# Two chained MLPs after a long convolution: the first MLP 20 tiles ahead of the second, weight decoding and GpSimd sums moved to other steps

## The chip, the cores and the metric

The kernel runs on one core of one Trainium2 chip. The metric is device time in microseconds (us): 2869.82 us, the median of three runs (2868.83 to 2870.09).

## The reference, cut to what matters

```
u = x * v;  h_filt = (relu(pos_emb @ w1) @ w2) * window
y = irfft(rfft(u, 2S) * rfft(h_filt, 2S))[:S];  a = x * y        # long convolution, S = 12480, 2 batches
g = h * clip(h + 3, 0, 6) / 6,   h = a @ w_in1;   b = g @ w_out1   # MLP 1, 24960 tokens, 128 -> 2048 -> 128
out = relu(b @ w_in2)**2 @ w_out2                                 # MLP 2, same sizes
```

All inputs are float32. The kernel is handed the four MLP weights as 64-bit words and makes float32 pairs of them on the chip ("decoding").

## The kernel before, in words

The first 497 us hold the filter MLP and the convolution, built as matrix products of a two-level Fourier transform. Their last level (`s4`, lines 451 to 464) is done tile by tile in the MLP part, which is the rest of the kernel and the part that is changed.

The 24960 tokens are 64 tiles of 390 tokens. Both MLPs go through all tiles; a tile of one MLP takes eight steps (q = 0 to 7), each with 256 of the 2048 hidden units. A list fixes the order of the steps (lines 478 to 486): MLP 1 (l = 0) starts AHEAD = 10 tiles early, then tiles of MLP 1 and MLP 2 (l = 1) alternate, and the last tiles are of MLP 2 alone. One loop (lines 612 to 639) issues each step's work to all engines; every engine runs its own instructions in the order in which they were issued.

One step is:
- `l1` (line 504): six matmuls, 128x128 weights by 390 tokens, into a PSUM tile `ph`. All operands are split in a high and a low part, so each product is three matmuls.
- `relu` (ScalarE, `r`) and `act` (VectorE, `g`, lines 531 and 534).
- `split`, one step later: ScalarE copies the high part `gh` (line 541), and VectorE or GpSimd subtracts for the low part `gl` (line 544). In the first 8*AHEAD steps VectorE takes this at q = 0, 3, 6 and GpSimd at the other five; after that VectorE has 0, 2, 4, 6.
- `l2`, three steps later (LAG): six matmuls into `acc`, the last two with `gl`.

`g` and `r` have two buffers each: the activation of step n can't write `g` before the split of step n-2 has read it. `acc` and the convolution's `py` share two PSUM buffers.

Around these: `finish` (line 568) takes a tile's result out of `acc`. For MLP 1 it makes the high part `xh` on ScalarE and the low part `xl` on VectorE (line 574), which wait in AHEAD + 1 buffers until MLP 2 comes to that tile. `combine` (line 433) makes the sums and differences for the convolution's last level: four GpSimd instructions, issued together at q = 5 of an MLP 1 tile while MLP 1 is alone, and at q = 2 of an MLP 2 tile later. `loads` issues the four DMAs of a later tile on SyncE's queue. `gate` and `gate_split` multiply by x and make `oh`, `ol` (line 475).

`late` (line 598) is a generator that decodes the weights still missing: 3 items are left of one part of the first output weights, 10 of another, and then for each weight of MLP 2 a DMA and 12 items of waiting, and four parts of 10 items: 117 items. Of a part's ten items eight are VectorE instructions on 512 columns (lines 100 to 119) and two are ScalarE's alone. The loop takes items ahead of `relu` and `act`: two a step up to n = 13, then five in four steps. They must be done when MLP 2 starts, at n = 88.

Of the kernel before, what the change touches and what calls it, by code (L numbers as in the profile page):

```python
# [7 lines left out]
F32 = mybir.dt.float32  # L8
F32R = mybir.dt.float32r
U32 = mybir.dt.uint32  # L10
AF = mybir.ActivationFunctionType
ALU = mybir.AluOpType
# [15 lines left out]
NT = 64  # L28
TOK = 390
# [10 lines left out]
def tile_hyena_moe(ctx: ExitStack, tc, xg, vg, xT, pos, w1d, w2d, win, fmat, twc,  # L40
                   tws, dcs, inv, vtab, w_in1, w_out1, w_in2, w_out2, out):
    nc = tc.nc
# [85 lines left out]
    def decode_split(w, part):  # L128
        for _ in parts.pop((w, part)):
            pass  # L130


    def tile_loads(j, za, zb, v, x):
        nc.sync.dma_start(v, vtab[j])
        nc.sync.dma_start(x, xT[j])
        nb = NBLK - (j == 0)
        for h, t in enumerate((za, zb)):
            zr = zds[0][h, j] if j < ZA else zds[1][h, j - ZA]
            nc.sync.dma_start(t.rearrange("k d r b c -> k d (r b c)")[:, :nb],
                              zr[:nb].rearrange("d k c -> k d c"))  # L140
# [215 lines left out]
    with tc.tile_pool(name="cv_ps", bufs=4, space=PSUM) as vps:  # L356
# [17 lines left out]
        for i in range(NI + 2):  # L374
# [26 lines left out]
            if i == NI - 1:  # L401
# [12 lines left out]
                za, zb = (room0[:K1, k].rearrange("k (d r b c) -> k d r b c", d=NBLK, r=2, b=2) for k in (0, 1))  # L414
# [8 lines left out]
    zt, pm, xin = {0: (za, zb)}, {}, {}  # L423

    def loads(j):
        za = mo.tile([K1, NBLK, 2, 2, 16], F32, name=f"za{j}", tag="za")
        zb = mo.tile([K1, NBLK, 2, 2, 16], F32, name=f"zb{j}", tag="zb")
        vt[j] = mo.tile([K1, 2, 2, N1], F32, name=f"vt{j}", tag="vt")
        xt[j] = mo.tile([128, TOK], F32, name=f"xt{j}", tag="xt")
        tile_loads(j, za, zb, vt[j], xt[j])  # L430
        zt[j] = (za, zb)

    def combine(j):
        za, zb = zt.pop(j)
        pp = mo.tile([K1, 2, 2, D], F32, name=f"pp{j}", tag="pp")
        pn = mo.tile([K1, 2, 2, D], F32, name=f"pn{j}", tag="pn")
        pm[j] = (pp, pn)

        p, n = (t.rearrange("k r b (d c) -> k d r b c", d=NBLK) for t in (pp, pn))
        if j == 0:  # L440
            for t, z in ((p, za), (n, zb)):
                for r in range(2):
                    nc.scalar.activation(t[:, :, r], z[:, :, r], AF.Copy)
            return
        for t, op in ((p, ALU.add), (n, ALU.subtract)):
            for r in range(2):
                nc.gpsimd.tensor_tensor(t[:, :, r], za[:, :, r], zb[:, :, 1 - r], op)  # L447

    py, ob = {}, {}

    def s4(j):

        ps = mps.tile([128, 512], F32, name=f"py{j}", tag="acc", bufs=2)
        v = vt.pop(j)
        for u in range(4):
            q, b = divmod(u, 2)
            o, n = UOFF[u]
            for r in range(2):
                nc.tensor.matmul(ps[:, o:o + n], pm[j][q][:, r, b, :],  # L459
                                 v[:, q, r, :n], start=(r == 0), stop=(r == 1))  # L460
                if u == 3 and r == 1:
                    pm.pop(j)
                    py[j] = ps
                yield

    def gate(j):
        ob[j] = mo.tile([128, TOK], F32, name=f"o{j}", tag="o")
        nc.vector.tensor_tensor(ob[j], py.pop(j)[:, :TOK], xt.pop(j), ALU.mult)

    def gate_split(j):  # L470
        o = ob.pop(j)
        h = mo.tile([128, TOK], F32R, name=f"oh{j}", tag="oh")
        l = mo.tile([128, TOK], F32R, name=f"ol{j}", tag="ol")
        nc.scalar.activation(h, o, AF.Copy)
        nc.vector.tensor_tensor(l, o, h.bitcast(F32), ALU.subtract)  # L475
        xin[(0, j)] = (h, l)

    AHEAD = 10
    order = []
    for j in range(NT + AHEAD):  # L480
        if j < NT:
            order.append((0, j))
        if j >= AHEAD:
            order.append((1, j - AHEAD))
    NP = NFC // 2
    steps = [(l, j, q) for l, j in order for q in range(NP)]
    LAG = 3
    QS = 4
    filling = {}

    def between(n, place):
# [6 lines left out]

        for _ in range(2 if j < AHEAD else place % 2):
            if "s4" in filling and next(filling["s4"], True):  # L500
# [3 lines left out]
    def l1(n):  # L504
        l, j, q = steps[n]
        xh, xl = xin[(l, j)]
        ps = mps.tile([128, 2, 512], F32, name=f"ph{n}", tag="ph", bufs=3)
        assert (2 * l, q // 2) in ready
        w = wh[2 * l]
        for c in range(2):  # L510
            f = 2 * q + c
            sl = slice(128 * f, 128 * f + 128)
            for m, (wt, x) in enumerate(((w[:, 1, sl], xh), (w[:, 0, sl], xl),
                                         (w[:, 0, sl], xh))):
                nc.tensor.matmul(ps[:, c, :TOK], wt, x, start=(m == 0), stop=(m == 2))  # L515
            between(n, c)
        ph[n] = ps
# [19 lines left out]
    def split(n):  # L537
# [3 lines left out]
        nc.scalar.activation(h, g, AF.Copy)  # L541
        on_vector = (0, 3, 6) if n < 8 * AHEAD else (0, 2, 4, 6)
        eng = nc.vector if steps[n][2] in on_vector else nc.gpsimd
# [3 lines left out]
    def l2(n):  # L547
        l, j, q = steps[n]
        if q == 0:
            acc[(l, j)] = mps.tile([128, 512], F32, name=f"acc{l}_{j}", tag="acc", bufs=2)  # L550
        ps = acc[(l, j)][:, :TOK]
        w = wh[2 * l + 1]
        h, lo = gh.pop(n)
        assert (2 * l + 1, q // 2) in ready
        ops = []
        for part, x in ((1, h), (0, h), (0, lo)):
            for c in range(2):
                f = 128 * (2 * q + c)
                ops.append((w[:, part, f:f + 128], x[:, c]))
        for m, (wt, x) in enumerate(ops):  # L560
            nc.tensor.matmul(ps, wt, x, start=(q == 0 and m == 0),  # L561
                             stop=(q == NP - 1 and m == len(ops) - 1))
            if m % 3 == 2:
                between(n + LAG, 2 + m // 3)
        if q == NP - 1:
            xin.pop((l, j))

    def finish(l, j):
        ps = acc.pop((l, j))[:, :TOK]
        if l == 0:  # L570
            h = mr.tile([128, TOK], F32R, name=f"xh{j}", tag="xh", bufs=AHEAD + 1)
            lt = mr.tile([128, TOK], F32R, name=f"xl{j}", tag="xl", bufs=AHEAD + 1)
            nc.scalar.activation(h, ps, AF.Copy, scale=1.0 / 6.0)
            nc.vector.scalar_tensor_tensor(lt, ps, 1.0 / 6.0, h.bitcast(F32),
                                           ALU.mult, ALU.subtract)
            xin[(1, j)] = (h, lt)
        else:
            ot = mr.tile([128, TOK], F32, name=f"ot{j}", tag="ot")
            nc.scalar.activation(ot, ps, AF.Copy)
            nc.scalar.dma_start(out[j], ot)  # L580

    loads(1)
    write(NBLK - 1, 1, tail.pop(), nc.sync)
    loads(2)
    staged.close()
    mr = ctx.enter_context(tc.tile_pool(name="moe2", bufs=2, side="right"))
    combine(0)
    for _ in s4(0):
        pass
    gate(0)  # L590
    gate_split(0)
    combine(1)
    decode_split(1, 0)
    for _ in range(2):
        next(parts[(1, 1)])
# [2 lines left out]
    def late():  # L598
        yield from parts.pop((1, 1))
        yield  # L600
        yield from decoding(None, 1, 2)
        yield
        for w in (2, 3):
            raw_weight(w)
            for _ in range(12):
                yield
            for part in range(4):
                yield from decoding(mr, w, part)
                yield

    rest = late()
    for n in range(len(steps) + LAG + 1):
        if n < len(steps):
            l, j, q = steps[n]
            l1(n)
        m = n - LAG
        if 0 <= m < len(steps):
            l2(m)
        if 0 <= m - 1 < len(steps) and steps[m - 1][2] == NP - 1:
            finish(*steps[m - 1][:2])  # L620
        if n < len(steps):
            if l == 0 and j < AHEAD and QS < q < QS + 3:
                (gate if q == QS + 1 else gate_split)(j + 1)
            if l == 1 and j + AHEAD + 1 < NT and q < 2:
                (gate_split if q else gate)(j + AHEAD + 1)
            for _ in range(2 if n < 14 or n % 4 == 0 else 1):
                next(rest, None)
            relu(n)
            act(n)
        if 0 <= n - 1 < len(steps):  # L630
            split(n - 1)
        if n < len(steps):

            t, at = (j, QS + 1) if l == 0 else (j + AHEAD, 2)
            if t < AHEAD or l == 1:
                if q == at and t + 2 < NT:
                    combine(t + 2)
                if q == at + 1 and t + 3 < NT:
                    loads(t + 3)


def _tables():
# [88 lines left out]
```

## Time and profile before

| | |
|---|---|
| median of three runs | 2869.82 us |
| the profiled execution | 2869.38 us, span 2867.6 us |
| TensorE busy with matmuls | 2779.6 us (97%), 15712 matmuls |
| VectorE / ScalarE / GpSimd busy | 2122.8 / 2006.1 / 1570.8 us |
| mean granted clock of TensorE | 0.991 |

Busy time is the time in which an engine has an instruction in work; a matmul's end is modelled. In the views, PE is TensorE (PEld its weight loads), DVE is VectorE, ACT is ScalarE, POOL is GpSimd and SP is SyncE; a trailing q is the engine's queue. L544 is line 544 of the kernel before. Windows are in us from the start of the span. An idle time is put down to what ended it, so "PEld acc <- POOL gl" is TensorE's time of waiting for GpSimd's `gl`.

### The profile page before, as it was taken

To read this page: it belongs to the slowest core of one execution; us is meant where nothing else is said; L and a number is where in the kernel's file an instruction comes from. 1 tells how busy PE (TensorE), PEld (TensorE's weight loads), DVE (VectorE), ACT (ScalarE), POOL (GpSimd) and SP (SyncE) were. 2 spreads that over 40 slices of the span, in tenths; PEclk is the share of its full clock that TensorE was granted. 3 is DMA by queue.
4 is the path that set the end of the run, shared out by engine and by line. 5 is a ranking of instruction groups with operands and counts; after the bars stand their busy time and mean duration, and the time that the engine had idled before them with its cause. 6 is when DMAs were issued, how large, how long until landed. Compare 5 with 4: busy or idle time off the path is not lost.

```text
span 2867.6 us, 42099 instructions
## 1 busy us (share of the span) xinstructions
PE 2779.6 (97%) x15712; PEld 2711.9 (95%) x15712; DVE 2122.8 (74%) x2280; ACT 2006.1 (70%) x2630; POOL 1570.8 (55%) x1020
## 2 busy tenths in 40 slices
PE   7999998888999999999999999999999999999999
PEld 5888887778999999999999999999999999999999
DVE  6888888899877777777777777777777777777666
ACT  6445445666777777777777777777777777777776
POOL 4888885655455555555555555555555555554444
PEclk9999999999999999999999999999999999999999
DMA  4343433321011111111110111111111111110000
GB/s 158 103 137 106 140 108 88 101 60 30 24 27 26 26 26 27 26 26 26 26 27 24 26 26 27 26 26 26 26 26 26 26 26 27 26 26 6 10 12 15
DMA packets 139419, 125.77 MB, mean 44 GB/s; under 512 B 99692, under 2 KB 122702, under 8 KB 137806
## 3 DMA queue, kind: packets, MB, share of 16 engines
q1 hardware_dynamic: 128322, 89.23, 11.4%
q10 hardware_dynamic: 10892, 33.86, 4.0%
q8 instruction: 123, 2.02, 0.3%
q14 instruction: 82, 0.67, 0.1%
HBM read 86.64 MB, written 36.37 MB: 43 GB/s over the span
## 4 chain that ended last, share of the span: by engine, by line
PE 83%; DVE 7%; issue 5%; ACT 2%; POOL 2%; DMA 0%; POOLq 0%; ACTq 0%; DVEq 0%
PE acc L561 36%; PE ph L515 36%; PE p L217 4%; PE py L459 3%; PE p L178 2%; PE p L248 1%; DVE g L531 1%; ACT h L331 1%; DVE a L194 1%; POOL l L203 1%; DVE b L188 1%; DVE p L192 1%; DVE wa L106 1%; DVE wa L104 0%; DVE gl L544 0%
## 5 line engine op out<-in xcount | busy, mean ns | idle before, releaser
L544 POOL TENSOR_TENSOR gl<-g,gh 128x780 fp32r<-128x780 f32 x522 | 984.2, 1885 | 1156.1 <-ACT gh L541 1151.5
L541 ACT ACTIVATE gh<-g 128x780 fp32r<-128x780 f32 x1024 | 869.1, 849 | 111.7 <-DVE g L531 61.9
L561 PE MATMUL acc<-gh,wp 128*128 128x390 f32 x4096 | 922.4, 347 | 6.3 <-DVE wp L119 6.3
L531 DVE SCALAR_TENSOR_TENSOR g<-r,ph 128x780 f32<-128x780 f32 x512 | 494.2, 966 | 350.8 <-POOL gl L544 285.8
L561 PEld LDWEIGHTS acc<-gh,wp 128*128 128x128 f32 x4096 | 729.6, 189 | 6.6 <-issue 6.6
L534 DVE SCALAR_TENSOR_TENSOR g<-ph,r 128x780 f32<-128x780 f32 x512 | 496.4, 970 | 277.8 <-POOL gl L544 244.1
L522 ACT ACTIVATE r<-ph,three 128x780 f32<-128x780 f32 x512 | 467.5, 913 | 254.5 <-PE ph L515 239.9
L515 PE MATMUL ph<-oh,wp 128*128 128x390 f32 x2048 | 635.7, 351 | 5.5 <-DVE g L531 4.2
L515 PE MATMUL ph<-xh,wp 128*128 128x390 f32 x2048 | 618.7, 343 | 0.0
L524 ACT ACTIVATE r<-ph 128x780 f32<-128x780 f32 x512 | 422.4, 825 | 235.8 <-PE ph L515 233.8
L561 PE MATMUL acc<-gl,wp 128*128 128x390 f32 x2048 | 537.9, 344 | 21.4 <-POOL gl L544 18.9
L544 DVE TENSOR_TENSOR gl<-g,gh 128x780 fp32r<-128x780 f32 x502 | 501.2, 998 | 0.6
L561 PEld LDWEIGHTS acc<-gl,wp 128*128 128x128 f32 x2048 | 372.9, 189 | 33.2 <-POOL gl L544 23.3
L515 PEld LDWEIGHTS ph<-oh,wp 128*128 128x128 f32 x2048 | 385.4, 191 | 7.7 <-DVE g L531 6.1
L515 PEld LDWEIGHTS ph<-xh,wp 128*128 128x128 f32 x2048 | 381.4, 189 | 0.0
L515 PE MATMUL ph<-ol,wp 128*128 128x390 f32 x1024 | 350.5, 342 | 0.0
L515 PE MATMUL ph<-xl,wp 128*128 128x390 f32 x1024 | 348.4, 340 | 0.0
L202 ACT ACTIVATE h<-a 128x720 fp32r<-128x720 f32 x96 | 76.7, 806 | 221.5 <-DVE a L194 133.8
L203 POOL TENSOR_TENSOR l<-a,h 128x720 fp32r<-128x720 f32 x96 | 168.0, 1750 | 94.1 <-ACT h L202 94.1
L515 PEld LDWEIGHTS ph<-ol,wp 128*128 128x128 f32 x1024 | 194.8, 190 | 0.3 <-DVE ol L475 0.3
L515 PEld LDWEIGHTS ph<-xl,wp 128*128 128x128 f32 x1024 | 192.6, 188 | 0.0
L447 POOL TENSOR_TENSOR pn<-za,zb 90x256 f32<-90x256 f32 x126 | 132.2, 1068 | 0.0
(90 smaller groups left out, 2711.0 us busy)
## 6 DMA issues: line engine op xcount, KB each, us to landing
zdb<-stg ACTq DMA_DIRECT2D x14, 1350.0 KB
x<-xg SPq DMA_DIRECT2D x64, 196.0 KB
v<-vg SPq DMA_DIRECT2D x64, 196.0 KB
out<-ot ACTq DMA_DIRECT2D x64, 195.0 KB
xt<-xT SPq DMA_DIRECT2D x63, 195.0 KB
za<-zdb SPq DMA_DIRECT2D x60, 180.0 KB
zb<-zdb SPq DMA_DIRECT2D x60, 180.0 KB
vt<-vtab SPq DMA_DIRECT2D x63, 137.8 KB
```

What stands on the lines that cost most here:

```text
L203: nc.gpsimd.tensor_tensor(l, gt, h.bitcast(F32), ALU.subtract)
L217: nc.tensor.matmul(pv, wt, x, start=(n == 0), stop=(n == len(ops) - 1))
L447: nc.gpsimd.tensor_tensor(t[:, :, r], za[:, :, r], zb[:, :, 1 - r], op)
L459: nc.tensor.matmul(ps[:, o:o + n], pm[j][q][:, r, b, :], v[:, q, r, :n], start=(r == 0), stop=(r == 1))
L515: nc.tensor.matmul(ps[:, c, :TOK], wt, x, start=(m == 0), stop=(m == 2))
L522: nc.scalar.activation(r, ph[n][:, :, :TOK], AF.Relu, bias=three)
L524: nc.scalar.activation(r, ph[n][:, :, :TOK], AF.Relu)
L531: nc.vector.scalar_tensor_tensor(g, r, 6.0, pv, ALU.min, ALU.mult)
L534: nc.vector.scalar_tensor_tensor(g, pv, 0.0, r, ALU.max, ALU.mult)
L541: nc.scalar.activation(h, g, AF.Copy)
L544: eng.tensor_tensor(l, g, h.bitcast(F32), ALU.subtract)
L561: nc.tensor.matmul(ps, wt, x, start=(q == 0 and m == 0), stop=(q == NP - 1 and m == len(ops) - 1))
```

## The change

AHEAD goes from 10 to 20, so that MLP 1 is alone for 20 tiles, VectorE's share of splits stays at three of eight until n = 159, and 20 tiles of MLP 2 are alone at the end. A waiting tile is kept as one float32 tile `x1`; its two parts are made by the new `part1` two steps before MLP 2 needs them. `combine` is a generator of two pairs, issued at q = 4 and 7 (MLP 1) or q = 1 and 3 (MLP 2). Decoding items go to the end of a step: two up to n = 13, then one, except at q = 5 and 6.

```diff
     def combine(j):
...
-        for t, op in ((p, ALU.add), (n, ALU.subtract)):
+        for k in range(2):
             for r in range(2):
-                nc.gpsimd.tensor_tensor(t[:, :, r], za[:, :, r], zb[:, :, 1 - r], op)
+                nc.gpsimd.tensor_tensor((p, n)[k][:, :, r], za[:, :, r], zb[:, :, 1 - r],
+                                        (ALU.add, ALU.subtract)[k])
+            yield
...
-    AHEAD = 10
+    AHEAD = 20
...
         if l == 0:
-            h = mr.tile([128, TOK], F32R, name=f"xh{j}", tag="xh", bufs=AHEAD + 1)
-            lt = mr.tile([128, TOK], F32R, name=f"xl{j}", tag="xl", bufs=AHEAD + 1)
-            nc.scalar.activation(h, ps, AF.Copy, scale=1.0 / 6.0)
-            nc.vector.scalar_tensor_tensor(lt, ps, 1.0 / 6.0, h.bitcast(F32),
-                                           ALU.mult, ALU.subtract)
-            xin[(1, j)] = (h, lt)
+            x1[j] = mr.tile([128, TOK], F32, name=f"x1{j}", tag="x1", bufs=AHEAD + 1)
+            nc.scalar.activation(x1[j], ps, AF.Copy, scale=1.0 / 6.0)
...
+    def part1(j):
+        x = x1.pop(j)
+        h = mr.tile([128, TOK], F32R, name=f"xh{j}", tag="xh")
+        lt = mr.tile([128, TOK], F32R, name=f"xl{j}", tag="xl")
+        nc.scalar.activation(h, x, AF.Copy)
+        nc.vector.tensor_tensor(lt, x, h.bitcast(F32), ALU.subtract)
+        xin[(1, j)] = (h, lt)
...
-            for _ in range(2 if n < 14 or n % 4 == 0 else 1):
-                next(rest, None)
+            if q == 6 and n + 2 < len(steps) and steps[n + 2][0] == 1:
+                part1(steps[n + 2][1])
             relu(n)
             act(n)
         if 0 <= n - 1 < len(steps):
             split(n - 1)
         if n < len(steps):
-            t, at = (j, QS + 1) if l == 0 else (j + AHEAD, 2)
+            t, at = (j, (4, 7)) if l == 0 else (j + AHEAD, (1, 3))
             if t < AHEAD or l == 1:
-                if q == at and t + 2 < NT:
-                    combine(t + 2)
-                if q == at + 1 and t + 3 < NT:
+                if q == at[0] and t + 2 < NT:
+                    sums = combine(t + 2)
+                if q in at and t + 2 < NT:
+                    next(sums)
+                if q == at[0] + 2 and t + 3 < NT:
                     loads(t + 3)
+
+            for _ in range(2 if n < 14 else int(q not in (QS + 1, QS + 2))):
+                next(rest, None)
```

## Rows read from the trace of the kernel before

**Rows 1.** The page: busy tenths of two engines in 40 slices of the span.
```profile
PE   7999998888999999999999999999999999999999
DVE  6888888899877777777777777777777777777666
```

**Rows 2.** Windows by stage: window, us, then busy us and (instructions) of each engine, PEclk, DMA.
```profile
497.18:755.97 258.79, 222.49 (x1214) 211.23 (x1215) 237.59 (x229) 167.69 (x225) 141.94 (x99) 0.96 0.22 59
755.97:2652.93 1896.96, 1896.92 (x10915) 1891.99 (x10914) 1347.73 (x1419) 1431.16 (x1839) 971.05 (x629) 1.00 0.10 26
2652.93:2867.60 214.67, 209.75 (x1171) 208.71 (x1170) 137.62 (x147) 157.87 (x208) 92.72 (x50) 1.00 0.03 12
```

**Rows 3.** Windows by tile, cut where a tile's first matmul starts; columns as before.
```profile
497.18:526.80 29.62, 20.13 (x94) 18.31 (x95) 29.40 (x28) 15.98 (x22) 17.97 (x14) 0.85 0.83 223
526.80:546.69 19.89, 19.89 (x113) 19.89 (x113) 12.81 (x15) 14.25 (x19) 9.04 (x6) 0.95 0.16 37
546.69:640.96 94.27, 80.27 (x449) 74.55 (x449) 90.68 (x87) 61.28 (x84) 53.15 (x37) 1.00 0.19 53
640.96:661.66 20.70, 19.18 (x114) 18.84 (x114) 13.36 (x14) 15.46 (x21) 12.38 (x10) 1.00 0.14 35
661.66:755.97 94.31, 83.01 (x449) 79.65 (x449) 91.33 (x88) 60.71 (x83) 49.41 (x35) 0.95 0.10 23
792.17:809.42 17.25, 17.25 (x99) 17.15 (x98) 13.96 (x15) 13.11 (x18) 9.81 (x8) 1.00 0.17 41
809.42:828.26 18.84, 18.84 (x113) 18.84 (x113) 11.57 (x13) 13.87 (x19) 8.71 (x5) 1.00 0.03 12
```

**Rows 4.** Waits from 497.18 to 755.97: who waited for whom, us, times, longest.
```profile
PEld acc L561 <- POOL gl L544: 21.4, 10, 2.5
...
PEld py L459 <- DVE xl L574: 8.2, 8, 1.1
...
PE acc L561 <- DVE wp L119: 6.3, 1, 6.3
```

**Rows 5.** GpSimd in order of time, a tile without decoding: start, us, instruction.
```profile
639.41 1.76 POOL L447 TENSOR_TENSOR pp<-za,zb 90x256 f32<-90x256 f32 x2
641.12 1.45 POOL L447 TENSOR_TENSOR pn<-za,zb 90x256 f32<-90x256 f32 x2
642.51 1.85 POOL L544 TENSOR_TENSOR gl<-g,gh 128x780 fp32r<-128x780 f32 x1
```

**Rows 6.** VectorE in order of time, right behind those.
```profile
644.39 0.97 DVE L531 SCALAR_TENSOR_TENSOR g<-r,ph 128x780 f32<-128x780 f32 x1 [3.65 <-POOL gl L544]
645.28 0.96 DVE L544 TENSOR_TENSOR gl<-g,gh 128x780 fp32r<-128x780 f32 x1
```

**Rows 7.** Tile 0 in order of time: a decoding instruction, and TensorE behind it.
```profile
520.89 3.68 DVE L119 TENSOR_TENSOR wp<-room 128x512 fp32r<-128x512 f32 x1
...
524.72 0.66 PE L561 MATMUL acc<-gh,wp 128*128 128x390 f32 x1 [6.35 <-DVE wp L119]
```

**Rows 8.** Single lines: duration ns min/median/max, first and last start, forms.
```profile
L106 DVE TENSOR_TENSOR wa<-wa,wg x8: 2132/2184/2245, 549.0 to 739.5; 128x512 f32<-128x512 f32 x8
...
L109 DVE TENSOR_SCALAR wm<-wa x8: 414/415/416, 552.8 to 742.5; 128x512 uint32<-128x512 uint32 x8
```

**Rows 9.** The parts of a tile: durations of lines 574, 475 and 468, same columns.
```profile
L574 DVE SCALAR_TENSOR_TENSOR xl<-acc,xh x64: 550/554/559, 535.5 to 2677.9; 128x390 fp32r<-128x390 f32 x64
...
L475 DVE TENSOR_TENSOR ol<-o,oh x64: 568/1930/1968, 497.2 to 2639.1; 128x390 fp32r<-128x390 f32 x64
...
L468 DVE TENSOR_TENSOR o<-py,xt x63: 556/557/561, 516.5 to 2637.3; 128x390 f32<-128x390 f32 x63
```

**Rows 10.** GpSimd and VectorE in order of time, where both MLPs alternate.
```profile
1379.56 1.44 POOL L447 TENSOR_TENSOR pp<-za,zb 90x256 f32<-90x256 f32 x2
...
1380.52 1.31 DVE L544 TENSOR_TENSOR gl<-g,gh 128x780 fp32r<-128x780 f32 x1
...
1380.97 2.16 POOL L447 TENSOR_TENSOR pn<-za,zb 90x256 f32<-90x256 f32 x2
```

**Rows 11.** Waits from 755.97 to 2652.93: the only one of TensorE.
```profile
PEld acc L561 <- POOL gl L544: 0.8, 3, 0.4
```

More of the change, by code (lines that the diff above doesn't have):

```diff
@@ L443, in combine @@
                     nc.scalar.activation(t[:, :, r], z[:, :, r], AF.Copy)
+                yield
             return
-        for t, op in ((p, ALU.add), (n, ALU.subtract)):
+        for k in range(2):
             for r in range(2):
-                nc.gpsimd.tensor_tensor(t[:, :, r], za[:, :, r], zb[:, :, 1 - r], op)
+                nc.gpsimd.tensor_tensor((p, n)[k][:, :, r], za[:, :, r], zb[:, :, 1 - r],
+                                        (ALU.add, ALU.subtract)[k])
+            yield
     py, ob = {}, {}
@@ L580, in finish @@
             nc.scalar.dma_start(out[j], ot)
+    x1 = {}
+    def part1(j):
[5 more added lines that the diff above has]
+        xin[(1, j)] = (h, lt)
     loads(1)
@@ L586, in tile_hyena_moe @@
     mr = ctx.enter_context(tc.tile_pool(name="moe2", bufs=2, side="right"))
-    combine(0)
-    for _ in s4(0):
-        pass
+    for f in (combine, s4):
+        for _ in f(0):
+            pass
     gate(0)
     gate_split(0)
-    combine(1)
+    for _ in combine(1):
+        pass
     decode_split(1, 0)
```

## The prediction

> **What bounds the kernel now.** I read the busy slices first [rows 1]: TensorE stands at nine tenths from the eleventh slice to the end. Before that it is lower in the first slice, which the change doesn't touch, and in slices 7 to 10, the end of the convolution and the start of the MLP part, where VectorE is at eight to nine tenths. So the MLP part has to be cut by stage [rows 2]. From 756 us to 2653 us, where both MLPs alternate, TensorE is busy for 1896.92 of 1896.96 us, at full clock: nothing that frees another engine can be worth anything there. Its only waits in that stretch are 0.8 us [rows 11]. The last stage is MLP 2 alone, 214.67 us, also on TensorE. The first stage, eleven tiles of MLP 1, has 258.79 us with TensorE busy for 222.49 and VectorE for 237.59.
>
> The windows by tile [rows 3] price that stage. A tile of MLP 1 that waits for nothing takes 18.84 us, one of MLP 2 17.25 us; the 1.6 us between them are the convolution's matmuls. The alternating stage holds 53 tiles of MLP 2 and 52 of MLP 1, so a mean MLP 1 tile there is (1896.96 - 53 x 17.25)/52 = 18.90 [rows 2]. I take 18.87. Eleven such tiles are 207.6 us, so the stage holds 258.8 - 207.6 = 51.2 us that another order could give back. By kind of tile:
> - tile 0: 29.62, 10.8 over the floor;
> - eight tiles in which a weight part is decoded, 94.27 + 94.31 = 188.6, or 23.57 each: 4.7 over, 37.6 together;
> - two tiles in which the decoder only waits for its DMA, 19.89 and 20.70: 1.0 and 1.8 over.
>
> In a decoding tile VectorE is busy for 22.7 to 22.8 of 23.6 us; in one that waits it is 12.8 to 13.4 [rows 3]. A part's ten items therefore cost VectorE about 22.7 - 13.1 = 9.6 us, or 0.96 us an item.
>
> **The change part by part.** *The order of tiles.* With 20 tiles ahead the counts stay: 64 tiles of either kind, each with its own floor. Ten more MLP 1 tiles move into the first stage and ten more MLP 2 tiles into the last. By itself this is worth 0; it buys time for decoding. Of 117 items 28 go in the first 14 steps as before; the other 89 now come at six in eight steps, 118.7 steps, and end near n = 133, in tile 16 and 27 steps ahead of MLP 2. Twelve of the 89 are the wait for the second weight, so 77 items make 77/6 = 12.8 decoding tiles where there were eight.
>
> *Decoding.* A decoding tile loses four of ten items, 3.8 us of VectorE, and `xl` (0.55 us [rows 9]), which goes to the MLP 2 tiles: 22.7 - 4.4 = 18.3 us of VectorE in an 18.9 us tile. That is full, but not over. What works against it: GpSimd's work a tile is unchanged (53.15/4 = 13.3 us [rows 3]), so its busy share rises from 13.3/23.6 = 56% to 70%, and items that meet it are the long ones. L106 took 2.13 to 2.25 us in all eight parts, though another 128x512 instruction, L109, took 0.41 [rows 8]. Also the items now stand behind `act` and the split, so an activation waits for the item of the step before. Bounds: if no item adds to TensorE's time, the tile is at 18.9 (0 over). If all seven of a part's eight VectorE instructions other than L109 take L106's 2.19 us, a part is 7 x 2.19 + 0.41 = 15.7 us, six items 9.4, and with 13.1 - 0.55 of the rest the tile is 22.0 (3.1 over). I take 20.0, 1.1 over: nearer the lower end, because the measured 0.96 an item already holds the collisions of a GpSimd at 56%. That is 12.8 x 1.1 = 14.1 us.
>
> The Trainium skill ("SBUF — State Buffer", section "Who interferes with whom") says that a VectorE instruction with two SBUF inputs and a GpSimd instruction that reads SBUF exclude each other for a whole instruction. L106 agrees, while `gate` on line 468, whose one input is PSUM, always took 0.56 [rows 9]. By that rule alone every colliding item would be a long one, and a decoding tile would go to the upper bound just given; this is rival B.
>
> *Sums in pairs.* In the tile without decoding GpSimd did four sums, 639.41 to 642.5, and only then the split that had become due meanwhile (642.51, 1.85 us) [rows 5]. VectorE's next `g` needed that split's buffer and sat idle for 3.65 us [rows 6], and TensorE waited for `gl`. Ten waits of TensorE for GpSimd's `gl` make 21.4 us in the stage [rows 4]. At q = 4 and 7 the split issued just before is VectorE's, so each pair (1.5 to 1.8 us) stands in a free slot of one 2.1 us step. This takes away what a tile without decoding loses: 1.0 to 1.8 becomes 0.1. New is that VectorE's own split now meets the pair. The nearest row: where a split met the sums it took 1.31 instead of 0.96, and the two sums behind it 2.16 instead of 1.44 [rows 10]. So 0.35 us of VectorE twice a tile, within the 20.0. A pair at q = 4 asks for its data one step sooner than now; they were loaded a tile before. The loads stay at the step where they were (q = 6, or q = 3 later), so SyncE's queue keeps its order; only the DMA for the second MLP 2 weight moves back with the decoder, and 12 items of waiting are then 16 steps, longer than before.
>
> *One float32 tile.* `finish` now has one ScalarE copy; `py` gets its PSUM buffer without VectorE's queue, where it waited eight times for `xl`, 8.2 us [rows 4]. This is inside the 4.7 a decoding tile loses, not a further gain. `part1` costs 64 more ScalarE copies, about 0.5 us each, and ScalarE is at 1431 of 1897 us [rows 2]. Its VectorE subtraction has two SBUF inputs like line 475, so 0.57 to 1.93 us instead of 0.55 [rows 9]: at most 1.4 us more on an engine that has 549 us idle over 53 tile pairs. Queued behind them are that step's `relu` and `act`. Both are hidden by the two steps (4.3 us) of matmuls between `part1` and the tile that reads them; without that cover it would be up to 1.4 us in each of 44 pairs.
>
> *Tile 0.* Its 10.8 us over the floor are mostly one wait: TensorE 6.35 us for the last instruction of a part, which took 3.68 us beside GpSimd's sums and split [rows 7]. Two sums are now earlier (q = 4), two later (q = 7), and the item is behind `act`. Bounds: the wait goes (4.4 over) or grows by one more GpSimd split, 1.85 us (12.7 over). I take 9.
>
> Sum over the floor: tile 0, 9.0; decoding 14.1; the other seven tiles of the 20-tile stage 0.1 each, 0.7; alternation and end as before. 23.8 against 51.2 is a gain of 27.4 us, from the profiled execution's 2869.4 us to 2842.0. The median lies 0.4 above that execution: 2842.4 us.
>
> **Rivals.** *A: the floor.* The items fit between the other work, decoding tiles are at 18.9 to 19.0. Then 9 + 1 to 2 remain over the floor: a gain of 40, 2829 us. For it: 18.3 us of VectorE in 18.9. Against: an engine at 97% with fixed order hardly hides all its collisions.
>
> *B: VectorE stays the bound.* Decoding tiles go to 22.0 and more: 9 + 12.8 x 3.1 + 0.7 = 49.4, a gain of 2, 2868 us; with activations queued behind long items and 22.6 a tile, 57, a loss of 6, 2876. For it: L106 in all eight parts and GpSimd at 70%. Against: the mean item is 0.96, not 2.2.
>
> *C: slower through the alternating stage.* There the pairs now meet VectorE's splits at q = 1 and 3 of every MLP 2 tile, right behind `ol` (1.93 us [rows 9]). A late split holds the next `g`, and then TensorE waits for `gl`. The price is up to one sum, 0.75 us, twice in the 42 MLP 2 tiles that issue sums: 63 us, less the 27 gained: 2905 us. It decides from 0.33 us a time on (27.4 us over 84 times). For it: that stage has no TensorE idle to absorb it. Against: the split of rows 10 met sums too, took only 0.35 us more, and TensorE did not wait [rows 11].
>
> **How the numbers follow.** Forecast 0.58 (2834 to 2856), A 0.20, B 0.15, C 0.07. The measurement tells 0.2%, 5.7 us, from no change: faster is below 2864. All of the forecast and A are faster; of B a third is faster, near a half same, the rest slower; C is slower but for a small part. Faster 0.84, same 0.07, slower 0.09. The range for 8 in 10 runs from the better half of A to the better end of B, 2829 to 2867.
>
> **What would show it.** Right: the first stage holds 21 tiles; tiles without decoding last 18.9 to 19.0 us; decoding ones near 20 with VectorE busy over 18; no `py` wait for `xl`; 36.1 us for a tile pair afterwards, as now. Wrong: decoding tiles over 21.5 (B), or TensorE waits for `gl` in the alternating stage that add up to more than 10 us (C), or a first tile over 31 us.

## The result and the profile after

The changed kernel takes 2830.67 us (median of four runs, 2828.38 to 2832.95), 38.7 us less than the kernel before in the same comparison (2869.32 us): a ratio of 0.9865, 95% interval 0.9848 to 0.9883. The profiled execution took 2832.95 us. The forecast was 2842.4 us with a range of 2829 to 2867: inside the range, but at its lower end, nearly the 2829 us of rival A. One run of e9 below took 5466.5 us, for a reason that no view shows, and is left out.

The stages of the changed kernel, columns as in [rows 2]; the first now holds 21 tiles of MLP 1, the second 43 tiles of MLP 2 and 42 of MLP 1, the third one tile of MLP 1 and 21 of MLP 2, where before it had one and 11:

```profile
499.31:911.91 412.60, 400.20 (x2335) 397.72 (x2335) 346.77 (x351) 310.10 (x406) 266.67 (x189) 0.99 0.21 55
911.91:2445.44 1533.53, 1533.53 (x8835) 1533.53 (x8834) 1107.17 (x1148) 1166.60 (x1531) 769.65 (x508) 1.00 0.10 25
2445.44:2831.10 385.66, 380.70 (x2131) 379.65 (x2130) 257.92 (x287) 295.41 (x398) 167.89 (x90) 1.00 0.04 12
```

At 18.87 us a tile the first stage has 412.6 - 21 x 18.87 = 16.3 us over the floor, where it had 51.2 with eleven tiles [rows 2]. That is 34.9 us of the gain. All that follows is 3.7 us shorter than before once the ten moved tiles are allowed for: 2111.6 us of the two later stages less 10 x 18.87, against 1919.2. The two executions differ by 2.1 us the other way in the convolution, which the change doesn't touch. The profiled execution is also the slowest of the four, 2.3 us above their median.

Single tiles of the first stage (tile 0; tile 1; tile 2; tiles 4 and 5, decoding; tiles 17 and 18, not decoding), to be read against [rows 3]:

```profile
499.31:529.30 29.99, 19.77 (x94) 18.27 (x95) 28.76 (x28) 16.08 (x22) 18.08 (x14) 0.84 0.79 220
529.30:548.95 19.65, 19.65 (x114) 19.65 (x113) 11.53 (x11) 14.34 (x19) 10.14 (x7) 0.96 0.15 37
548.95:569.76 20.81, 19.19 (x113) 18.86 (x113) 19.60 (x21) 14.68 (x20) 12.77 (x10) 1.00 0.14 33
588.76:626.65 37.89, 37.89 (x225) 37.89 (x225) 35.76 (x36) 29.91 (x40) 25.79 (x19) 1.00 0.17 40
836.18:874.12 37.94, 37.94 (x225) 37.94 (x225) 26.76 (x26) 28.12 (x38) 24.36 (x19) 1.00 0.17 38
```

A tile that decodes six items takes the same 18.95 us as one that decodes none, with VectorE busy for 17.9 us of it. What is left over the floor is tile 0 (11.1 us), tile 2 (1.9), tile 1 (0.8), tiles 6 and 13 (0.6 each) and 1.2 us in all the others. In tile 1 TensorE never waits (19.65 us busy of 19.65): its granted clock is 0.96, at the lower of its two levels (1.2 GHz) for the first 1.5 us behind tile 0's long wait. Some of TensorE's waits in the stage, to be read against [rows 4]:

```profile
PEld acc L565 <- issue: 8.3, 1, 8.3
PE acc L565 <- DVE wp L119: 8.0, 1, 8.0
...
PEld ph L519 <- DVE ol L479: 2.3, 2, 1.9
...
PEld acc L565 <- POOL gl L548: 1.3, 1, 1.3
...
PEld py L463 <- ACT x L577: 1.2, 2, 0.6
```

Tile 0's wait for a decoding instruction is now the largest. The wait for GpSimd's `gl` was 21.4 us in ten places and is 1.3 in one; that of `py` for `xl` is gone, with 1.2 us for the new copy on ScalarE in its place. In the alternating stage TensorE has no wait at all in the view.

### The profile page after: what moved, and what is told of

Read it like the earlier page. It is cut to its first block, busy times and chain, and to the rows that moved or that the text cites. A ratio compares the mean times of both kernels' runs of the same rounds, so it can differ in the third digit from the quotient of the medians.

```text
span 2831.1 us, 42236 instructions
## 1 busy us (share of the span) xinstructions
PE 2765.9 (98%) x15712; PEld 2712.0 (96%) x15712; DVE 2112.1 (75%) x2270; ACT 2021.9 (71%) x2694; POOL 1569.1 (55%) x1030
## 4 chain that ended last, share of the span: by engine, by line
PE 88%; DVE 4%; issue 3%; POOL 2%; ACT 2%; DMA 1%; ACTq 0%; POOLq 0%; SPq 0%; DVEq 0%
PE acc L565 38%; PE ph L519 38%; PE p L217 4%; PE py L463 4%; PE p L178 2%; PE p L248 1%; DVE a L194 1%; POOL l L203 1%; DVE b L188 1%; DVE p L192 1%; POOL a L241 0%; ACT h L331 0%; POOL v L155 0%; POOL a L194 0%; DVE b L236 0%
## 5 line engine op out<-in xcount | busy, mean ns | idle before, releaser
L548 POOL TENSOR_TENSOR gl<-g,gh 128x780 fp32r<-128x780 f32 x532 | 1006.1, 1891 | 1114.3 <-ACT gh L545 1109.4
L545 ACT ACTIVATE gh<-g 128x780 fp32r<-128x780 f32 x1024 | 866.6, 846 | 15.1 <-DVE g L535 13.1
L548 DVE TENSOR_TENSOR gl<-g,gh 128x780 fp32r<-128x780 f32 x492 | 516.1, 1049 | 0.0
L479 DVE TENSOR_TENSOR ol<-o,oh 128x390 fp32r<-128x390 f32 x64 | 118.4, 1850 | 10.2 <-ACT oh L478 10.2
```

The lines of the kernel that those rows point to most:

```text
L548: eng.tensor_tensor(l, g, h.bitcast(F32), ALU.subtract)
```

## The experiments

Three theories: 1, the rate of decoding is what counts (six items a tile leave VectorE room, ten don't); 2, the items' place in the step is; 3, the sums in pairs carry a gain of their own. Times are medians; each ratio is to the kernel before as timed in the same comparison (2868.5 to 2869.7 us). The last column is the first stage's time over 18.87 us a tile (21 tiles, or 11 with ten ahead), read from each profile as above.

| run | change to which kernel | us | ratio to before, interval | over the floor |
|---|---|---|---|---|
| before | | 2869.3 | | 51.2 |
| after | all | 2830.7 | 0.9865 [0.9848, 0.9883] | 16.3 |
| e1 | after, 10 ahead, old rate | 2848.0 | 0.9923 [0.9908, 0.9938] | 31.6 |
| e2 | after, items first | 2830.8 | 0.9868 [0.9853, 0.9882] | 16.1 |
| e3 | after, four sums together | 2867.7 | 0.9995 [0.9985, 1.0004] | 51.1 |
| e4 | after, loads ahead of the write | 2830.0 | 0.9865 [0.9849, 0.9882] | 15.1 |
| e5 | before, pairs alone | 2856.2 | 0.9955 [0.9939, 0.9972] | 39.6 |
| e6 | after, an item in every step | 2843.5 | 0.9910 [0.9895, 0.9925] | 27.2 |
| e7 | after, four sums at q = 7 | 2853.8 | 0.9949 [0.9934, 0.9964] | 37.2 |
| e8 | e4 and fewer double steps | 2829.4 | 0.9863 [0.9848, 0.9877] | 14.8 |
| e9 | before, pairs and float32 tile | 2851.4 | 0.9934 [0.9915, 0.9954] | 36.1 |
| e10 | after, items first, sums together | 2873.3 | 1.0015 [1.0006, 1.0024] | 59.4 |

**e1, ten tiles ahead.**
```diff
-    AHEAD = 20
+    AHEAD = 10
...
-            for _ in range(2 if n < 14 else int(q not in (QS + 1, QS + 2))):
+            for _ in range(2 if n < 14 or n % 4 == 0 else 1):
```


> The changed kernel with AHEAD = 10 and the old rate of decoding (five items in four steps after n = 13, done by n = 88); items stay at the end of the step, sums in pairs, one float32 tile. Theory 1 (the rate: six items a tile leave VectorE room, ten don't): in the changed kernel two tiles without decoding have 26.8 us of VectorE and two with six items 35.8, so 0.75 us an item; ten items make 13.4 + 7.5 = 20.9 us in an 18.9 us tile, eight tiles at 21 to 22, 17 to 25 us lost: 2848 to 2856 us. Theory 2 (the place in the step is what counts): at most 5 us lost, 2830 to 2836 us.

17.4 us lost, as theory 1 said. Tiles 3 to 5 (ten items each) and tile 6, which waits for its DMA:

```profile
570.07:632.77 62.70, 59.18 (x337) 56.36 (x337) 62.09 (x62) 46.14 (x62) 41.91 (x28) 1.00 0.24 69
632.77:651.72 18.95, 18.95 (x113) 18.95 (x113) 12.10 (x14) 14.61 (x21) 11.36 (x10) 1.00 0.16 41
```

The decoding tiles take 20.9 us, VectorE (the third engine of the row) works 62.09/3 = 20.7 of them; the tile beside them is at the floor. Tiles 8 and 9 are longer, 21.5 us each with VectorE at 19.9, so its whole work is not all that counts there.

**e2, items ahead of the activation.**
```diff
+            for _ in range(2 if n < 14 else int(q not in (QS + 1, QS + 2))):
+                next(rest, None)
             if q == 6 and n + 2 < len(steps) and steps[n + 2][0] == 1:
...
-            for _ in range(2 if n < 14 else int(q not in (QS + 1, QS + 2))):
-                next(rest, None)
```


> The changed kernel with its items taken ahead of relu and act, as before, at the same rate of six in eight steps. Theory 1 (the rate): no loss, 2828 to 2834 us. Theory 2 (the place): an item that waits for GpSimd holds the activation of its own step, decoding tiles go to 20 or more, 12.8 tiles lose 1.1 us or more each: 2845 us or more.

No loss: with the sums in pairs and six items a tile the place is worth nothing in the sum, and theory 2 falls for the changed kernel. Single tiles do move: tiles 3, 7, 14 and 15 take 19.5 us instead of 19.0, while tile 0 is 0.6 us shorter and tile 2 is 1.3.

**e3, four sums together.**
```diff
-            t, at = (j, (4, 7)) if l == 0 else (j + AHEAD, (1, 3))
+            t, at = (j, QS + 1) if l == 0 else (j + AHEAD, 2)
...
-                if q == at[0] and t + 2 < NT:
-                    sums = combine(t + 2)
-                if q in at and t + 2 < NT:
-                    next(sums)
-                if q == at[0] + 2 and t + 3 < NT:
+                if q == at and t + 2 < NT:
+                    for _ in combine(t + 2):
+                        pass
+                if q == at + 1 and t + 3 < NT:
```


> The changed kernel with the four sums of a tile issued together again, at q = 5 (MLP 1) and q = 2 (MLP 2). Theory 3 (the pairs carry a gain of their own): each of some 18 tiles of the first stage loses the 1.0 to 1.8 us that tiles without decoding lost before, 2848 to 2863 us. Theory 1 (the rate is all): up to 5 us lost, 2830 to 2836 us. Either way the alternating stage stays at 36.1 us a tile pair.

37 us lost, nearly the whole gain, more than even theory 3 had. Tiles 17 to 19, where nothing is decoded any more:

```profile
863.64:926.00 62.36, 57.72 (x338) 56.75 (x337) 38.13 (x39) 42.97 (x56) 37.46 (x28) 1.00 0.14 35
```

20.8 us a tile with VectorE at 61%: VectorE has room and TensorE waits all the same. GpSimd, and then VectorE, from tile 15 to tile 16 of e3:

```profile
839.54 1.90 POOL L548 TENSOR_TENSOR gl<-g,gh 128x780 fp32r<-128x780 f32 x1 [3.19 <-ACT gh L545]
841.40 1.76 POOL L449 TENSOR_TENSOR pp<-za,zb 90x256 f32<-90x256 f32 x2
843.12 1.45 POOL L449 TENSOR_TENSOR pn<-za,zb 90x256 f32<-90x256 f32 x2
844.53 1.82 POOL L548 TENSOR_TENSOR gl<-g,gh 128x780 fp32r<-128x780 f32 x1
```
```profile
846.39 0.97 DVE L535 SCALAR_TENSOR_TENSOR g<-r,ph 128x780 f32<-128x780 f32 x1 [3.65 <-POOL gl L548]
```

It is the picture of [rows 5, 6], to the same 3.65 us. The same place in the changed kernel, from tile 4 to tile 5: two splits at the steps' pace, then one pair in the slot of VectorE's split.

```profile
604.31 1.88 POOL L548 TENSOR_TENSOR gl<-g,gh 128x780 fp32r<-128x780 f32 x1 [2.07 <-ACT gh L545]
606.46 1.88 POOL L548 TENSOR_TENSOR gl<-g,gh 128x780 fp32r<-128x780 f32 x1 [0.27 <-ACT gh L545]
608.29 1.43 POOL L449 TENSOR_TENSOR pn<-za,zb 90x256 f32<-90x256 f32 x2
```

**e5, the pairs alone in the kernel before** (`combine` as in the change, at q = 4 and 7, 1 and 3).

> The kernel before with the sums in two pairs (q = 4 and 7, later 1 and 3) and nothing else. In the run with the sums together every tile of the first stage lost 1.8 us in its first step, decoded or not. Theory 3 (the pairs remove that loss from ten tiles, ten items a tile still fill VectorE): 18 us gained, 2849 to 2854 us, and decoding tiles at 21 to 22 us. Theory 1 (the rate is all): no gain, 2865 us or more.

12.2 us gained, less than the 18 expected. Tile 6, which doesn't decode, falls from 20.70 to 18.95 us; the decoding tiles only from 23.6 to 22.4. In tiles 2 to 4 VectorE is busy for 21.8 of 22.2 us, and about 1 us of each is the wait of `py` for `xl` (next run).

**e9, the pairs and the float32 tile.** Like e1, but with the items ahead of `relu` and `act`.

> The kernel before with the pairs and the float32 tile alone: AHEAD = 10, the old rate of decoding, items ahead of relu and act. The run with the pairs alone (items first, parts made in finish) took 2856 us, the one with ten tiles ahead (pairs, float32 tile, items last) 2848 us. Theory x (the 8 us between them are the eight waits of py for xl, 1.05 us each, that the float32 tile takes away): 2845 to 2851 us, q = 4 of decoding tiles at 3.85 instead of 4.9 us. Theory y (they come from the items' place behind act): 2853 to 2858 us, with q = 4 at 3.85 and the time lost in other steps.

2851.4 us, just above theory x's band. The step q = 4 went from 4.9 to 3.86 us as it said, but other steps gave back part, so the tile is worth 4.9 us (e5 to e9; 6.1 if each run is set against the kernel before of its own comparison), 3.5 of it in the first stage. The place is worth the other 3.3 (e9 to e1) where ten items a tile overfill VectorE. Two rows of e5 show the wait that the tile removes; e9 has no such entry:

```profile
PEld py L461 <- DVE xl L576: 8.4, 8, 1.1
...
PE py L461 <- DVE xl L576: 5.8, 8, 0.8
```

**e10, all of the change but the pairs and the place.**

> The kernel before with 20 tiles ahead, the float32 tile and six decoding items in eight steps, but items first and the four sums together. Theory (without the pairs the longer first stage loses on ten more tiles what slower decoding gains): 1.8 us in each of 20 tiles and 11 in tile 0, 2862 to 2870 us, as the kernel before. Rival (items first leave GpSimd's late split more cover): 2845 us or less.

2873.3 us, 0.15% slower than before and above the theory's band. Without the pairs the longer first stage is worth less than nothing: it spreads the decoding, but also gives ten more tiles the 1.8 us of the sums. Tiles 3, 7, 8, 14 and 15 take 22.7 to 22.8 us, 1.9 more than in e3, where the items stand behind `act`. With the sums together the place therefore does count, 5.6 us between e3 and e10.

**e6, an item in every step.**
```diff
-            for _ in range(2 if n < 14 else int(q not in (QS + 1, QS + 2))):
+            for _ in range(2 if n < 14 else 1):
```


> The changed kernel with one decoding item in every step, q = 5 and 6 too: eight a tile, 11 decoding tiles. Theory (VectorE's time a tile is the limit): 13.4 + 8 x 0.75 = 19.4 us against 18.9, so decoding tiles at 19.4 to 20.2 us and 5 to 14 us lost, 2835 to 2845 us. Rival (there is room up to ten items, and the loss with ten came from elsewhere): 2828 to 2833 us.

12.9 us lost. Tiles 3 to 6, eight items each, take 20.35 us; VectorE's work is 78.48/4 = 19.6 us a tile, more than the floor's 18.9:

```profile
570.32:651.73 81.41, 78.33 (x449) 75.12 (x449) 78.48 (x76) 60.63 (x81) 53.53 (x37) 1.00 0.22 62
```

That is twice the excess, and VectorE's work is not the only cause, as tile 13 shows. It has one item left:

```profile
770.41:790.62 20.21, 19.25 (x114) 18.92 (x114) 16.01 (x16) 14.23 (x20) 12.70 (x10) 1.00 0.16 38
```

VectorE works 16.0 us in it, and it still takes 20.21. Its first step waits for `ol`, behind the item of q = 5, a step that e6 added, and then `ol` itself is long:

```profile
767.84 1.67 DVE L117 TENSOR_TENSOR wa<-wa,wp 128x512 f32<-128x512 f32 x1
769.43 2.23 DVE L479 TENSOR_TENSOR ol<-o,oh 128x390 fp32r<-128x390 f32 x1
```

Tiles 4 and 9 begin in the same way: three first steps of 3.3 to 3.4 us instead of 2.15, some 3.6 of the 10.9 us that the first stage lost. So the expectation's number came, but by this reading about a third of it from the place of the item at q = 5 and not from VectorE's time a tile. No run has eight items a tile in other steps.

**e7, four sums at q = 7.**
```diff
-                if q == at[0] and t + 2 < NT:
-                    sums = combine(t + 2)
-                if q in at and t + 2 < NT:
-                    next(sums)
+                if q == at[1] and t + 2 < NT:
+                    for _ in combine(t + 2):
+                        pass
```


> The changed kernel with all four sums in one place again, but at q = 7 (MLP 1) and q = 3 (MLP 2), where the split just issued is VectorE's. Theory a (what cost 1.8 us was a GpSimd split standing behind one split and four sums; here the next GpSimd split is issued one step later and is late by only 3.3 + 1.5 - 3.9, about 0.9 us, which the lag of three steps covers): 2828 to 2835 us. Theory b (four sums in a row are too long for any one place): most of the 1.8 us a tile comes back, 2850 to 2867 us.

The time lies in theory b's band, but neither theory holds for every tile. Tiles that decode nothing are at 19.1 us, so the late split is covered, as theory a had it; tiles that decode mostly take 20.3 to 21.5, so 23 of the 37 us come back. VectorE from the split of tile 15's last step on, then GpSimd beside it:

```profile
835.99 1.31 DVE L548 TENSOR_TENSOR gl<-g,gh 128x780 fp32r<-128x780 f32 x1
837.22 3.48 DVE L109 TENSOR_SCALAR wm<-wa 128x512 uint32<-128x512 uint32 x1
840.62 0.95 DVE L535 SCALAR_TENSOR_TENSOR g<-r,ph 128x780 f32<-128x780 f32 x1
```
```profile
836.43 2.16 POOL L449 TENSOR_TENSOR pn<-za,zb 90x256 f32<-90x256 f32 x2
838.55 1.87 POOL L548 TENSOR_TENSOR gl<-g,gh 128x780 fp32r<-128x780 f32 x1
```

The decoding item behind the split lasted 3.48 us, to the end of sums and split, although L109 took 0.41 us in all eight parts before [rows 8]. The activation behind it waited. L109 lasted 3.5 us in three of the eight parts of this run, this one included.

**e4 and e8, what is left.** Tile 0's 8 us: L117 stood 4.83 us behind sums that had waited 4.64 us for tile 2's data, whose loads stand behind the convolution's last write. Tile 2's 1.9 us: the two items of n = 13 stand ahead of `ol`. Both runs have the first edit, e8 alone has the second.

```diff
     loads(1)
-    write(NBLK - 1, 1, tail.pop(), nc.sync)
     loads(2)
+    write(NBLK - 1, 1, tail.pop(), nc.sync)
...
-            for _ in range(2 if n < 14 else int(q not in (QS + 1, QS + 2))):
+            for _ in range(2 if n < 12 else int(q not in (QS + 1, QS + 2))):
```


> The changed kernel with the loads of tile 2 issued ahead of the last write of the convolution (two DMAs of 1350 KB) on SyncE's queue. In the changed kernel TensorE waits 8.05 us in tile 0 for a decoding instruction that stood 4.83 us behind sums which themselves had waited 4.64 us for tile 2's data, and the first step of tile 2 takes 4.03 instead of 2.14 us. Theory (that data is late because it stands behind the write): the sums run before the split of q = 4, tile 0 loses 3 to 6 us less and tile 2 up to 1.9 us less: 2823 to 2828 us. Rival (the transfers share the same 16 engines, so the order is worth nothing): 2829 to 2833 us.

> The changed kernel with the loads of tile 2 ahead of the write, and two items a step only up to n = 11 instead of 13. In the changed kernel the two items of n = 13 (2.1 us each beside GpSimd) stand ahead of gate_split's subtraction, and the first step of tile 2 waits for it: 4.03 instead of 2.14 us. Theory: that 1.9 us goes, with up to 1.4 us in tile 0: 2827 to 2829 us, just under the changed kernel. Rival (the wait moves to another tile): 2829 to 2832 us.

In e4 the sums no longer wait for data and tile 0 takes 28.6 us, 1.4 less, but the item still comes late; the median moved by 0.6 us, inside the noise. In e8 tile 2 is at the floor:

```profile
546.32:565.23 18.91, 18.91 (x113) 18.91 (x113) 17.92 (x18) 15.18 (x21) 12.74 (x10) 1.00 0.16 39
```

Tiles 6 and 13 lost 0.4 us each and tile 1 0.6, as the rival had it. At 2829.4 us e8 can't be told from the changed kernel.

## Why the prediction was right, and where a term was off

- **Where the time lay** held: all but 3.7 us of the gain came out of the first stage, and the alternating stage stayed on TensorE. That nothing could be gained there was not quite so: its MLP 2 tiles went from 17.27 to 17.22 us, about 2 us together, though the view had TensorE busy throughout.
- **Sums in pairs.** The mechanism was read rightly from [rows 5, 6], and e3 shows it undone. Its weight was not: I gave it the tiles without decoding and left it inside the 20.0 us elsewhere. It is 1.7 to 2.4 us in each of the tiles 2 to 20 (34.8 us between the first stages of e3 and the changed kernel), and without it the rest of the change gains next to nothing (e3, e10). One of the two tiles that it was to help was misread: tile 1 waited for nothing before either, 19.89 us busy of 19.89 at a granted clock of 0.95 [rows 3], and kept 0.8 of its 1.0 us.
- **Decoding** is the mis-sized term: 14.1 us over the floor forecast, 4.0 measured in the 13 tiles that decode (2 to 7 and 10 to 16), 1.9 of it from the doubled items ahead of tile 2. The VectorE sum was near (18.3 us forecast, 35.76/2 = 17.9 measured); an item costs 0.75 us, (35.76 - 26.76)/12, not 0.96. That the sum came so near is in part luck: it left 18.3 - 6 x 0.96 = 12.5 us for the rest of the tile, which is 13.4, so that two errors cancel. Wrong was the 1.1 us put on top because an engine near 97% with a fixed order should show through. In the changed kernel a tile with 17.9 us of VectorE's work takes TensorE's 18.9 us. Where the work is more than that, the tile takes at least as long: 20.9 us for 20.7 and 21.5 for 19.9 (e1), 20.35 for 19.6 (e6). Less work alone doesn't make it free, as e6's tile 13 shows. Forecast and measured work both lay below the floor, which is rival A.
- **The total.** That it comes within 2 us of rival A is in part luck: A left 10 to 11 us over the floor, 16.3 were measured, and 3.7 us came out of later tiles that neither A nor the forecast had.
- **Rival B** did not come. Items that met GpSimd were long, as read, but six items cost 6 x 0.75 = 4.5 us a tile and not 9.4: L106 took 0.68 us in three of the changed kernel's eight parts and 1.5 to 1.7 in the others.
- **Order of tiles**, worth 0 by itself: no run has the order alone. With slower decoding and the float32 tile, but without the pairs and the new place, it is 4 us worse than before (e10). With the pairs, the order and the slower decoding that it allows are worth 17 us (e1). A small slip: MLP 2 starts at n = 168, so the items end 35 steps ahead of it, not 27.
- **One float32 tile.** `py` no longer waits for `xl`, as forecast; it waits 1.2 us in two places for the new copy, in tiles 6 and 13. `part1` is hidden; its subtraction took 0.56 us in all 64 cases, and no GpSimd instruction ran beside it in any of them, so the dearer bound of 1.93 never came.
- **Tile 0**: 9 forecast, 11.1 measured. The item came later, not earlier: the sums moved to q = 4 met data that hadn't landed, a wait I had ruled out. e4, where they don't wait, gives back 1.4 us.
- **Rival C** did not come: no wait of TensorE in that stage.

What stays open: part of the 3.7 us in the MLP 2 tiles (below), which item places would let more than six items a tile through, and what share of e5's missing gain is VectorE's time and what its order.

## What to carry to other kernels

Read an in-order helper engine by slots: a burst of background work belongs in the step whose main work another engine does, and in pieces no longer than the slot. Here that alone decided whether the rest of the change was worth 37 us or nothing; where nothing was decoded, the right step was enough even for all four sums (19.1 us a tile in e7). Compare, tile by tile, an engine's whole work with the bottleneck's: with three steps of lag 17.9 us beside 18.9 cost nothing, and 19.6 us cost more than the excess. So stretching background work over more tiles pays until it fits. Then look at the single steps too: an item ahead of something that TensorE needs at once, as `ol` in e6, costs time however much room the tile has.

## What the runs showed of the hardware that was not expected

A VectorE instruction with one input can be held as a two-input one is: L109 took 0.41 us in eight cases before [rows 8] and 3.48 us beside sums and a split in e7. The prediction set L109 against L106 as if their kinds made the difference. In the trace of the kernel before it is what GpSimd does when they start: each L106 began 0.24 to 0.55 us into a split of GpSimd, and no L109 began while GpSimd was at work. L102, with one input like L109, shows both: 0.42 us in four parts, and 1.87 us in the four in which it began inside a split. The first two rows are L102 and the split around its start, the last two L109 and the split that came just behind its start:

```profile
663.46 1.83 POOL L544 TENSOR_TENSOR gl<-g,gh 128x780 fp32r<-128x780 f32 x1
663.70 1.88 DVE L102 TENSOR_SCALAR wa<-wa 128x512 uint32<-128x512 uint32 x1
...
552.79 0.41 DVE L109 TENSOR_SCALAR wm<-wa 128x512 uint32<-128x512 uint32 x1
552.96 2.00 POOL L544 TENSOR_TENSOR gl<-g,gh 128x780 fp32r<-128x780 f32 x1 [2.40 <-ACT gh L541]
```

In the changed kernel every second MLP 2 tile is shorter at the same full clock and without a wait, 17.10 against 17.26 us for the fourth and the fifth:

```profile
1020.34:1037.44 17.10, 17.10 (x99) 17.10 (x98) 14.14 (x14) 12.89 (x18) 10.10 (x8) 1.00 0.18 42
1056.29:1073.55 17.26, 17.26 (x99) 17.26 (x98) 14.16 (x14) 13.13 (x19) 10.09 (x8) 1.00 0.22 42
```

The tile's two parts lie in two buffers in turn there, in eleven before. The mean over the MLP 2 tiles is 17.19 us against 17.25 before and 17.22 with the pairs alone (e5); over 63 tiles that makes the 3.7 us, but the buffers are not the whole of it. In the alternating stage the mean is 17.27 before, 17.23 in e5 and 17.22 in the changed kernel; in e3, which has the two buffers and not the pairs, it is 17.28 and the pattern is gone. In the last stage, where no sums run, a tile takes 17.15 before and 17.13 in e3 and the changed kernel, with the pattern in both (17.07, 17.22, 17.04, 17.19 one after another), and ten more tiles stand there. So most of the 3.7 us goes with the pairs and with the ten tiles' new stage. That the pattern comes from where the parts lie is not shown.
